# Sums of p.v as three additions and of pooled v as two, each in place of one strided pass, in a fused attention and two-layer kernel

## The chip, the cores and the metric

The kernel runs on one core of a Trainium2 chip. A core has a matrix engine (TensorE; PE in the profile), a vector engine (VectorE, DVE), a scalar engine (ScalarE, ACT), a general engine (GpSimd, POOL) and a queue for transfers (SyncE, SP). Each engine works through its own queue strictly in order. The metric is device time in microseconds (us), as a median over runs.

## The reference

Inputs are q, k and v of 4 batches, 8 heads, 576 positions and 64 dimensions. Cut to what matters:

```python
q_d, k_d, v_d = means of q, k, v over groups of 4 positions   # 144 positions
out_up    = repeat(softmax(q_d k_d^T / 8) v_d, 4)             # pooled attention
mask      = abs(i - j) < 4                                    # 7 neighbours
out_local = softmax(where(mask, q k^T / 8, -1e9)) v           # local attention
x = (out_up + out_local) as 2304 tokens x 512
h = x @ w_in                                                  # first layer, 2048 wide
x = (max(h, 0) + alpha * min(h, 0)) @ w_out
xn = x / sqrt(mean(x*x) + 1e-6) * rms_g                       # second layer, 1536 wide
out = (silu(xn @ w_gate) * (xn @ w_val)) @ w_out2
```

## The kernel before

The 2304 tokens are six blocks (m = 0 to 5) of 384, each of two groups of 192 tokens (g = 0 to 11). Every product of the two layers is made of three fp16 matmuls (high times high, high times low, low times high). `m1` runs the first layer on a block: per step f of 16, 24 matmuls of 384 columns (`hps` at L1368, `acc` at L1385), and on DVE the rows `hps` (L1374) and `ghl` (L374). `m2` runs the second layer: per step of 12, 24 matmuls for `gps` (L1485) and 9 for `oacc` (L1514), and on DVE `th` (L1496), `gps` (L1499) and `uhl` (L1506). ScalarE makes one pass between each of these. The blocks run in the order m1(0), m1(1), m2(0), m2(1), m1(2), m1(3), m2(2), m2(3), m1(4), m1(5), m2(4), m2(5).

The attention of a batch has to be done before the first layer takes its tokens, so it is fed as background tasks into the layers' steps. There are two ways of doing the local part. The first 768 tokens (groups 0 to 3) go over TensorE (the classes `Dense` and `DenseHead`). Groups 4 to 11 go over DVE and GpSimd, in `local_tasks`: positions lie in partitions, and six units per group (two positions times two heads of a pair each) are worked off one after another. For each unit, `mul_qk` multiplies q with seven neighbours' k (896 products per partition, tile `prod`), `red_qk` sums them over the dimension into `ls` (L489); after the softmax (`sm1`, `sm2`, last row L520) `mul_av` multiplies the weights with seven neighbours' v (L526, again 896 products in a `prod` tile), and `red_av` sums the seven into `lo` (L544). The products of units 0, 2 and 4 are made by GpSimd, those of units 1, 3 and 5 by DVE (the string "GVGVGV"). There are two buffers for `prod`, so a product waits until the unit two before it is summed. At the end `trans` turns `lo` over TensorE (`xps`, L560), adds the pooled attention (L573) and splits the sum into fp16 halves in `xt`.

The pooled attention of batch 0 is in `Dense.down`. Its first task, `smm`, sums four neighbouring rows of v (tile `sdv`, 72 partitions) into the part `pv` of a `dd` tile, with one reduction at L806. The other batches go through `down_tasks`, whose `pool` does the same with two additions (L632, L634).

The order of the queues isn't that of the code. `issue_order` (L24) takes all instructions, gives each a duration by a formula on its shape, and plans all engines forwards and backwards in 40 rounds; the order of the best round is laid on each engine. Its formula for DVE is 89 ns and a nanosecond or half of one per element, and 60 more for a scalar operand. The plan also lets a DVE instruction with two operands in SBUF and a GpSimd instruction wait for each other. So an edit of one instruction makes the order of all engines anew.

The two places that the change touches are, in the kernel before:

```python
add(st["o"][:, t:t + TP, j], pr[:, :, 0], pr[:, :, 2])            # L542, third of three, if av_pool
nc.vector.tensor_reduce(out=st["o"][:, t:t + TP, j],
    in_=pr.rearrange("p t n d -> p t d n"), axis=AX.X, op=ALU.add)  # L544, otherwise
def local(g, mul="GVGVGV", av=False, ...)                          # L1607: av is av_pool
```

Of the kernel before, what the change touches and what calls it, by code (L numbers as in the profile page):

```python
# [13 lines left out]
ALU = mybir.AluOpType  # L14
AX = mybir.AxisListType
# [240 lines left out]
def kernel(  # L256
# [14 lines left out]
    nc = tc.nc  # L271
    B, H, S, D = q.shape
# [23 lines left out]
    @contextmanager  # L296
    def together():
        n = len(nc.cur_bb.bb.instructions)
        yield
        groups.append([i.name for i in nc.cur_bb.bb.instructions[n:]])  # L300
# [413 lines left out]
    def pool_of(tag):  # L714
        return {"raw": raw_p, "xt": xt_p, "hl": hl_p, "ob": ob_p, "prod": prod_p, "at": ps_t, "w": ps_w}.get(
            tag) or (ps_a if tag in ("a0", "a1", "a2", "a3") else x1_p if tag[0] in "xr" and tag != "xs" else
                     wts if tag[0] in "uw" else att)

    class Dense:
# [78 lines left out]
        def down(self, h):  # L798
            st = self.st[h]

            def smm():
                t = st["qkp"]
                buf = prod_p.tile([SH, 4 * SD + 4 * D], F32, tag="prod", name="dd")
                a_ = buf[:, 0:4 * SD].rearrange("p (j a k) -> p j a k", j=2, a=2)
                st["pv"] = buf[:, 4 * SD:4 * SD + 4 * D].rearrange("p (j a d) -> p j a d", j=2, a=2)
                nc.vector.tensor_reduce(out=st["pv"].rearrange("p j a d -> p (j a) d"),  # L806
                                        in_=st.pop("v").rearrange("p (g r d) -> p g d r", g=4, r=4), axis=AX.X, op=ALU.add)
                ps = [pool_of(self.smp[j]).tile([128, 2, SD], F32, tag=self.smp[j], name="sps") for j in range(2)]
                with together():
                    for a in range(2):  # L810
                        for j in range(2):
                            nc.tensor.matmul(
                                ps[j][0:SH, a], t[j * 64:j * 64 + 64, 0, a * SH:(a + 1) * SH],
                                t[j * 64:j * 64 + 64, 1, :], start=True, stop=True)
                m = att.tile([SH, 2, 2], F32, tag=f"dm{h % 2}", name="dm")
                sm = att.tile([SH, 2, 2], F32, tag=f"dsum{h % 2}", name="dsum")
                for j in range(2):
                    nc.vector.tensor_reduce(out=m[:, j], in_=ps[j][0:SH], axis=AX.X, op=ALU.max, negate=True)
                nc.vector.tensor_scalar(out=m, in0=m, scalar1=1.0 / 16.0, scalar2=None, op0=ALU.mult)
                for j in range(2):  # L820
                    for a in range(2):
                        nc.scalar.activation(out=a_[:, j, a], in_=ps[j][0:SH, a], func=AF.Exp, scale=1.0 / 16.0,
                                             bias=m[:, j, a:a + 1], accum_out=sm[:, j, a:a + 1])
                st["a"], st["sum"] = a_, sm

            def nrm():
                a_, sm = st["a"], st["sum"]
                nc.vector.tensor_scalar(out=sm, in0=sm, scalar1=1e-9, scalar2=4.0, op0=ALU.add, op1=ALU.mult)
                nc.vector.reciprocal(sm, sm)
                nc.gpsimd.tensor_tensor(out=a_, in0=a_, in1=sm.unsqueeze(3).to_broadcast([SH, 2, 2, SD]),  # L830
                                        op=ALU.mult)

            def atr():
                t = att.tile([SH, 2, 2 * SD], F32, tag=("aT", "lo")[h % 2], name="aT")
                for j in range(2):
                    ps = ps_t.tile([128, 2 * SD], F32, tag="at", name="atps")
                    for kh in range(2):
                        for qh in range(2):
                            o = kh * SD + qh * SH
                            nc.tensor.transpose(ps[0:SH, o:o + SH], st["a"][:, j, qh, kh::2], ident[0:SH, 0:SH])  # L840
                    nc.scalar.activation(out=t[:, j], in_=ps[0:SH], func=AF.Copy)
                st["aT"] = t

            def avm():
                ps = ps_t.tile([128, SD], F32, tag="at", name="avps")
                with together():
                    for kh in range(2):
                        for j in range(2):
                            nc.tensor.matmul(ps[j * 64:j * 64 + 64, :], st["pv"][:, j, kh],
                                             st["aT"][:, j, kh * SD:(kh + 1) * SD], start=(kh == 0), stop=(kh == 1))  # L850
                if h == 0:
                    outd_t[self.b] = outd_p.tile([128, HP, SD], F32, tag="outd", name="outd")
                st["od"] = outd_t[self.b][:, h]
                nc.scalar.activation(out=st["od"], in_=ps, func=AF.Copy)

            return [smm, nrm, atr, avm]

        def local(self, c, h0, banks):
# [745 lines left out]
    def flush():  # L1604
        run(len(urgent), len(bg))

    def local(g, mul="GVGVGV", av=False, tags=(None, None, None), **kw):  # L1607
        return local_tasks(g, [V if c == "V" else G for c in mul], tags, av, **kw)

    def down(b, n=3, **kw):  # L1610
# [59 lines left out]
    def cut(l, at):  # L1670
# [8 lines left out]
        "o1": [],  # L1679
        "c3": pr2[2],  # L1680
        ("m2", 0): weave(pr2[3],local(4)),
        ("m2", 1): local(5)+down(2)+local(6),
        ("m1", 2): local(7)+local(8),
        ("m1", 3): down(3)+local(9),
        ("m2", 2): local(10),
# [57 lines left out]
```

## Time and profile before

| what | value |
|---|---|
| median of 3 runs | 993.3 us (991.09 to 995.36) |
| profiled execution | 989.59 us, its span 987.9 us |
| TensorE, weights of TensorE | 934.8 us (95%), 600.0 us (61%) busy |
| DVE, ScalarE, GpSimd | 695.7 (70%), 480.6 (49%), 117.1 us (12%) busy |
| transfers | 73.79 MB, 75 GB/s on average |

The span is the time from the first to the last instruction of one execution under the profiler. A row's duration runs from its start to its end; on DVE the next row starts a little before the last one ends, so the sum of durations is somewhat over the busy time. A matmul's duration contains its way through the array, so that 22 matmuls of 0.33 us each follow one another in 3.58 us. "Idle before" names what an engine waited for, as far as the semaphores show it.

### The profile page before, as it was taken

Reading aid. Unit: us, or ns where it says so; the run is one execution under the profiler, and the core shown is the slowest. Engines: PE = TensorE matmul, PEld = TensorE weight load, DVE = VectorE, ACT = ScalarE, POOL = GpSimd, SP = SyncE. Lnnn points to the kernel's source line nnn. Section 1 sums busy time; section 2 is a strip of 40 time slices with the busy share of each in tenths; the row PEclk is TensorE's granted clock in tenths of the full one; section 3 lists DMA queues with packets and bytes.
Section 4 is the critical chain, followed back from the end, with each engine's and each line's share of the span. In section 5 each row is a group of like instructions: output and inputs, shape, how many; then the busy total and the mean of one; then the engine's idle time right before and its main releaser. Section 6 shows DMA issues by size and latency. Waiting matters only on the chain.

```text
span 987.9 us, 16462 instructions
## 1 busy us (share of the span) xinstructions
PE 934.8 (95%) x6484; PEld 600.0 (61%) x6484; DVE 695.7 (70%) x1347; ACT 480.6 (49%) x1108; POOL 117.1 (12%) x96
## 2 busy tenths in 40 slices
PE   6978899999999999899899999989999999999998
PEld 4667777699655555455566555545556666555554
DVE  5689996888999977999976899953343353442333
ACT  5899889789753264233376322221232432321322
POOL 1101100300210202332201223300000000000000
PEclk9999999999999999999999999999999999999999
DMA  8866534565111133121122121010000000000000
GB/s 220 273 210 192 150 93 145 193 213 172 66 48 56 34 120 106 66 70 56 37 75 91 50 72 39 3 31 1 11 22 1 1 1 1 1 1 3 30 1 33
DMA packets 53711, 73.79 MB, mean 75 GB/s; under 512 B 22190, under 2 KB 35138, under 8 KB 53634
## 3 DMA queue, kind: packets, MB, share of 16 engines
q1 hardware_dynamic: 53634, 72.74, 24.2%
q8 instruction: 51, 0.84, 0.3%
q14 instruction: 26, 0.21, 0.1%
HBM read 68.01 MB, written 4.72 MB: 74 GB/s over the span
## 4 chain that ended last, share of the span: by engine, by line
PE 62%; DVE 18%; ACT 13%; DMA 4%; issue 3%; SPq 0%; ACTq 0%; DVEq 0%
PE gps L1485 20%; PE acc L1385 13%; PE hps L1368 12%; PE oacc L1514 9%; DVE lo L544 6%; DMA out_dram<-ob 3%; ACT wr L1107 2%; DVE prod L526 2%; ACT dls L897 2%; ACT wr L1110 1%; DVE gps L1499 1%; DVE hps L1374 1%; ACT g L1372 1%; ACT wi L373 1%; DVE ghl L374 1%
## 5 line engine op out<-in xcount | busy, mean ns | idle before, releaser
L1368 PE MATMUL hps<-xt,wi 128*128 128x192 f16 (+1 forms) x1536 | 342.7, 289 | 8.3 <-DVE ghl L374 5.1
L1485 PE MATMUL gps<-x,w 128*128 128x384 f16 x1728 | 341.2, 327 | 6.6 <-DVE th L1496 5.8
L1385 PE MATMUL acc<-ghl,wo 128*128 128x384 f16 (+1 forms) x960 | 246.0, 311 | 4.3 <-ACT ghl L373 3.2
L1485 PEld LDWEIGHTS <-w 128*128 128x128 f16 x1728 | 169.7, 99 | 120.8 <-issue 10.0
L1514 PE MATMUL oacc<-w,uhl 128*128 128x512 f16 x630 | 190.0, 379 | 1.7 <-ACT ob L1570 1.4
L1368 PEld LDWEIGHTS <-wi 128*128 128x128 f16 x1536 | 147.9, 100 | 57.0 <-issue 4.5
L1385 PEld LDWEIGHTS <-wo 128*128 128x128 f16 x1344 | 127.8, 98 | 67.0 <-issue 9.8
L1374 DVE SCALAR_TENSOR_TENSOR hps<-g,oma,hps 128x192 f32<-128x192 f32 (+1 forms) x128 | 65.9, 517 | 68.2 <-ACT g L1372 67.4
L1496 DVE SCALAR_TENSOR_TENSOR th<-th,gps 128x384 f32<-128x384 f32 x72 | 39.6, 551 | 96.5 <-ACT th L1494 96.1
L1514 PEld LDWEIGHTS <-uhl 128*128 128x128 f16 x630 | 61.9, 98 | 70.1 <-issue 4.8
L1494 ACT ACTIVATE th<-gps,tsc 128x384 f32<-128x384 f32 x72 | 41.7, 579 | 121.6 <-PE gps L1485 121.4
L1505 ACT ACTIVATE uhl<-gps 128x384 f16<-128x384 f32 x72 | 41.6, 578 | 109.0 <-DVE gps L1499 87.4
L1372 ACT ACTIVATE g<-hps 128x384 f32<-128x384 f32 x96 | 47.2, 492 | 91.8 <-PE hps L1368 91.3
L544 DVE TENSOR_REDUCE lo<-prod 128x128 f32<-128x896 f32 x48 | 82.4, 1719 | 0.0
L478 POOL TENSOR_TENSOR prod<-cq,ckv 128x896 f32<-128x896 f32 x24 | 52.3, 2179 | 198.4 <-DMA ckv<-in_k_dram 48.8
L373 ACT ACTIVATE ghl<-hps,grp 128x384 f16<-128x384 f32 (+1 forms) x73 | 42.1, 578 | 55.3 <-DVE hps L1374 54.1
L1385 PE MATMUL acc<-g,wo 128*128 128x384 f16 (+1 forms) x384 | 67.5, 286 | 0.0
L1506 DVE TENSOR_TENSOR uhl<-gps,uhl 128x384 f16<-128x384 f32 x72 | 45.3, 629 | 30.3 <-ACT uhl L1505 30.1
L526 POOL TENSOR_TENSOR prod<-ls,ckv 128x896 f32<-128x896 f32 x24 | 44.2, 1844 | 161.0 <-DVE lo L544 66.5
L374 DVE SCALAR_TENSOR_TENSOR ghl<-hps,grp,ghl 128x384 f16<-128x384 f32 (+1 forms) x73 | 44.3, 607 | 22.4 <-ACT ghl L373 22.2
L489 DVE TENSOR_REDUCE ls<-prod 128x14 f32<-128x896 f32 x48 | 51.1, 1074 | 0.0
L1107 ACT ACTIVATE wr<-wr 128x768 f32<-128x768 f32 (+1 forms) x48 | 42.2, 882 | 2.6 <-DMA wr<-in_moe_w_out_dram 2.6
(240 smaller groups left out, 1121.1 us busy)
## 6 DMA issues: line engine op xcount, KB each, us to landing
wr<-in_moe_w_out_dram SPq DMA_DIRECT2D x18, 512.0 KB
wr<-in_moe_w_in_dram SPq DMA_DIRECT2D x10, 768.0 KB
wr<-in_moe_w_gate_dram SPq DMA_DIRECT2D x8, 768.0 KB
wr<-in_moe_w_val_dram SPq DMA_DIRECT2D x8, 768.0 KB
ckv<-in_k_dram SPq DMA_DIRECT2D x7, 768.0 KB
ckv<-in_v_dram SPq DMA_DIRECT2D x7, 768.0 KB
wr<-in_moe_w_out_dram SPq DMA_DIRECT2D x20, 256.0 KB
sd<-in_q_dram SPq DMA_DIRECT2D x24, 144.0 KB
```

Source lines behind the costliest of these rows:

```text
L373: nc.scalar.activation(out=hi, in_=src, func=AF.Copy, scale=s)
L374: nc.vector.scalar_tensor_tensor(out=lo, in0=src, scalar=s, in1=hi, op0=ALU.mult, op1=ALU.subtract)
L478: engs[i].tensor_tensor(out=pr, in0=view(st["q"][:, j, t:t + TP], [[D, TP], [0, ND], [1, D]]), in1=view(st["k"][:, j, t:t + TP], [[D, TP], ...
L526: engs[i].tensor_tensor(out=pr, in0=view(st["s"][:, j, t:t + TP], [[ND, TP], [1, ND], [0, D]]), in1=view(st["v"][:, j, t:t + TP], [[D, TP] ...
L544: nc.vector.tensor_reduce(out=st["o"][:, t:t + TP, j], in_=pr.rearrange("p t n d -> p t d n"), axis=AX.X, op=ALU.add)
L1107: nc.scalar.activation(out=hi.bitcast(F32), in_=hi.bitcast(F32), func=AF.Prelu, scale=2.0 ** -112, alpha=2.0 ** 32)
L1368: nc.tensor.matmul(ps[:, j], wi[:, f + j, a, kk * 128:(kk + 1) * 128], x[:, b_, kk, c0:c0 + n], start=(i == 0), stop=(i == 3 * KK - 1))
L1372: nc.scalar.activation(out=g, in_=ps, func=AF.Relu, scale=-1.0)
L1374: nc.vector.scalar_tensor_tensor(out=ps[:, j], in0=g[:, j], scalar=oma[:, f + j:f + j + 1], in1=ps[:, j], op0=ALU.mult, op1=ALU.add)
L1385: nc.tensor.matmul(acc[e], wo_f(f)[:, a, e * 128:(e + 1) * 128], hl[:, b_], start=(f == f0 and i == 0), stop=(f == f1 and i == 2))
L1485: nc.tensor.matmul(ps, w2_t[i0 + f // 3].rearrange("p a (k c) -> p a k c", k=KK)[:, a, kk, (f % 3) * 128:(f % 3 + 1) * 128], xh[:, b_, kk] ...
L1514: nc.tensor.matmul(acc[tt], t[:, a, tt * 128:(tt + 1) * 128], w[:, b_, f % 3], start=(f in first and i == 0), stop=(f in last and i == 2))
```

## The change

Three things are edited. `local` has `av=True` as its default, so `red_av` takes its first branch: in the product tile of seven slices of 64, slices 0 to 2 get slices 3 to 5 added (384 elements per partition), then slices 0 and 2 get slices 1 and 6 added (256), and the third addition writes slice 0 plus slice 2 into `lo` (128). All three read two operands in SBUF. In `Dense.down` the reduction L806 becomes two additions, of 512 and of 256 elements per partition, the first in place in the tile of v. And since the instructions are others, the order is planned anew. Lines after L806 have numbers that are higher by three in the kernel after.

```diff
-                nc.vector.tensor_reduce(out=st["pv"].rearrange("p j a d -> p (j a) d"),
-                                        in_=st.pop("v").rearrange("p (g r d) -> p g d r", g=4, r=4), axis=AX.X, op=ALU.add)
+                vt = st.pop("v").rearrange("p (g r) -> p g r", g=4)
+                nc.vector.tensor_tensor(out=vt[:, :, 0:2 * D], in0=vt[:, :, 0:2 * D], in1=vt[:, :, 2 * D:4 * D],
+                                        op=ALU.add)
+                nc.vector.tensor_tensor(out=st["pv"].rearrange("p j a d -> p (j a) d"), in0=vt[:, :, 0:D],
+                                        in1=vt[:, :, D:2 * D], op=ALU.add)
...
-    def local(g, mul="GVGVGV", av=False, tags=(None, None, None), **kw):
+    def local(g, mul="GVGVGV", av=True, tags=(None, None, None), **kw):
```

What `red_av` now runs stands in both kernels:

```python
add = lambda o, a, c: nc.vector.tensor_tensor(out=o, in0=a, in1=c, op=ALU.add)
add(pr[:, :, 0:3], pr[:, :, 0:3], pr[:, :, 3:6])
add(pr[:, :, 0:3:2], pr[:, :, 0:3:2], pr[:, :, 1:7:5])
add(st["o"][:, t:t + TP, j], pr[:, :, 0], pr[:, :, 2])
```

The first place where the order is shown is DVE's queue in the fourth of the eight groups (g = 7, inside m1(2)). Of the kernel before, from unit 1's product on; `prod_5473`, `prod_5506`, `prod_5510` and `prod_5513` are units 0 to 3, and the rows L526 are the products that DVE makes itself:

```order
L526 TENSOR_TENSOR prod_5506<-ls_5367,ckv_5432 128x896
L544 TENSOR_REDUCE lo_5508<-prod_5473 128x2x64
L374 SCALAR_TENSOR_TENSOR xt_5295<-xs_5302,sc_104,xt_5295 128x4x96
L544 TENSOR_REDUCE lo_5508<-prod_5506 128x2x64
L1374 SCALAR_TENSOR_TENSOR hps_5517<-g_5530,oma_102,hps_5517 128x384
L526 TENSOR_TENSOR prod_5513<-ls_5367,ckv_5432 128x896
L544 TENSOR_REDUCE lo_5508<-prod_5510 128x2x64
L374 SCALAR_TENSOR_TENSOR ghl_5516<-hps_5517,grp_115,ghl_5516 128x384
L544 TENSOR_REDUCE lo_5508<-prod_5513 128x2x64
```

And of the kernel after, where `prod_5513`, `prod_5546`, `prod_5552` and `prod_5557` are units 0 to 3 (L1377 is L1374 of before):

```order
L526 TENSOR_TENSOR prod_5546<-ls_5407,ckv_5472 128x896
L539 TENSOR_TENSOR lo_5548<-prod_5513 128x2x64
L539 TENSOR_TENSOR prod_5546<-prod_5546 128x2x192
L374 SCALAR_TENSOR_TENSOR ghl_5515<-hps_5516,grp_115,ghl_5515 128x384
L1377 SCALAR_TENSOR_TENSOR hps_5563<-g_5576,oma_102,hps_5563 128x384
L539 TENSOR_TENSOR prod_5546<-prod_5546 128x2x2x64
L539 TENSOR_TENSOR prod_5552<-prod_5552 128x2x192
L539 TENSOR_TENSOR lo_5548<-prod_5546 128x2x64
L539 TENSOR_TENSOR prod_5552<-prod_5552 128x2x2x64
L526 TENSOR_TENSOR prod_5557<-ls_5407,ckv_5472 128x896
```

Each sum has become three rows, and between them stand rows of the first layer (`hps`, `ghl`). The second row of the later piece is the third addition of unit 0, which frees the buffer for GpSimd's product of unit 2.

The second place is the end of the last group's sums (g = 11, inside m2(3)), DVE's queue. Before:

```order
L526 TENSOR_TENSOR prod_7957<-ls_7617,ckv_7758 128x896
L1499 SCALAR_TENSOR_TENSOR gps_7554<-th_7551,kap_119,gps_7554 128x384
L544 TENSOR_REDUCE lo_7862<-prod_7912 128x2x64
L1506 TENSOR_TENSOR uhl_7568<-gps_7554,uhl_7568 128x384
L544 TENSOR_REDUCE lo_7862<-prod_7957 128x2x64
```

After, where L1499, L1502 and L1509 are the rows L1496, L1499 and L1506 of before:

```order
L526 TENSOR_TENSOR prod_8053<-ls_7705,ckv_7846 128x896
L1499 SCALAR_TENSOR_TENSOR th_7771<-th_7771,gps_7758 128x384
L539 TENSOR_TENSOR lo_7950<-prod_8006 128x2x64
L1502 SCALAR_TENSOR_TENSOR gps_7774<-th_7771,kap_119,gps_7774 128x384
L539 TENSOR_TENSOR prod_8053<-prod_8053 128x2x192
L539 TENSOR_TENSOR prod_8053<-prod_8053 128x2x2x64
L1509 TENSOR_TENSOR uhl_7788<-gps_7774,uhl_7788 128x384
L539 TENSOR_TENSOR lo_7950<-prod_8053 128x2x64
```

There are three rows of the second layer between the last own product and the last write of `lo`, where two stood before. GpSimd's queue keeps its products in the same sequence.

## Rows read from the trace of the kernel before

**Rows 1.** The page, busy time of each engine, and DVE in 40 slices.
```profile
PE 934.8 (95%) x6484; PEld 600.0 (61%) x6484; DVE 695.7 (70%) x1347; ACT 480.6 (49%) x1108; POOL 117.1 (12%) x96
...
DVE  5689996888999977999976899953343353442333
```

**Rows 2.** Three stretches: length; busy PE, PEld, DVE, ACT, POOL; clock; transfers' share; GB/s.
```profile
0.00:235.00 235.00, 211.55 (x2062) 174.18 (x2063) 190.65 (x473) 201.36 (x512) 26.61 (x50) 0.99 0.62 187
235.00:655.00 420.00, 396.85 (x2515) 238.26 (x2513) 382.00 (x652) 183.88 (x423) 90.47 (x47) 1.00 0.21 64
655.00:987.90 332.90, 326.44 (x1912) 187.52 (x1909) 123.07 (x225) 95.31 (x174) 0.00 (x0) 1.00 0.03 9
```

**Rows 3.** The same for eight stretches, one per group: second, third, last, sum.
```profile
320.50:342.50 22.00, 20.36 (x119) 11.64 (x117) 22.00 (x32) 3.72 (x7) 5.18 (x3) 1.00 0.07 21
397.20:418.00 20.80, 18.20 (x101) 9.54 (x100) 20.68 (x23) 3.98 (x8) 8.03 (x5) 1.00 0.15 52
...
631.50:652.00 20.50, 17.80 (x100) 9.62 (x98) 20.23 (x23) 5.09 (x9) 5.07 (x3) 1.00 0.10 26
sum 200.60, PE 178.59 PEld 108.20 DVE 194.68 ACT 78.63 POOL 56.05; mean PE 22.32 PEld 13.53 DVE 24.34 ACT 9.83 POOL 7.01
```

**Rows 4.** DVE in order of time in the third group: start, length, row.
```profile
398.58 1.68 DVE L526 TENSOR_TENSOR prod<-ls,ckv 128x896 f32<-128x896 f32 x1
400.18 1.71 DVE L544 TENSOR_REDUCE lo<-prod 128x128 f32<-128x896 f32 x1
401.81 0.61 DVE L1499 SCALAR_TENSOR_TENSOR gps<-th,kap,gps 128x384 f32<-128x384 f32 x1
402.34 1.73 DVE L544 TENSOR_REDUCE lo<-prod 128x128 f32<-128x896 f32 x1
403.99 0.54 DVE L1506 TENSOR_TENSOR uhl<-gps,uhl 128x384 f16<-128x384 f32 x1
```

**Rows 5.** TensorE at the end of that group, idle before in brackets.
```profile
417.62 0.32 PE L1368 MATMUL hps<-xt,wi 128*128 128x384 f16 x1 [2.32 <-DVE ghl L374]
```

**Rows 6.** Groups by line and shape: count | busy us, mean ns | idle before.
```profile
L544 DVE TENSOR_REDUCE lo<-prod 128x128 f32<-128x896 f32 x48 | 82.4, 1719 | 0.0
...
L632 DVE TENSOR_TENSOR sd<-sd 72x512 f32<-72x512 f32 x36 | 25.2, 699 | 4.6 <-ACT dd L619 4.6
...
L1299 DVE TENSOR_TENSOR ra<-ra 128x384 f32<-128x384 f32 x15 | 8.3, 553 | 1.1 <-ACT ra L1294 1.1
...
L806 DVE TENSOR_REDUCE dd<-sdv 72x256 f32<-72x1024 f32 x4 | 7.7, 1936 | 0.0
...
L573 DVE TENSOR_TENSOR xs<-xps,outd 128x128 f32<-128x128 f32 x16 | 6.0, 373 | 0.0
...
L634 DVE TENSOR_TENSOR dd<-sd 72x256 f32<-72x256 f32 x12 | 5.0, 417 | 0.0
```

**Rows 7.** The chain of waits in the first 60 us, shares by line.
```profile
by line: PE lsps L877 10.4%; PE tps L792 9.9%; ACT T L793 9.2%; ACT dls L897 8.0%; ACT dls L912 6.5%; ACT dd L822 6.3%; PE atps L840 6.1%; ACT wr L1107 6.0%; DMA wo<-in_q_dram 5.8%; PE sps L812 5.6%; SPq L743 4.4%; PE avps L849 4.1%; PE lsp
```

**Rows 8.** GpSimd in order of time: two p.v products.
```profile
401.97 1.69 POOL L526 TENSOR_TENSOR prod<-ls,ckv 128x896 f32<-128x896 f32 x1 [2.66 <-DVE lo L544]
...
468.94 1.94 POOL L526 TENSOR_TENSOR prod<-ls,ckv 128x896 f32<-128x896 f32 x1 [9.48 <-issue]
```

**Rows 9.** DVE in order of time beside the second of them.
```profile
468.72 0.61 DVE L374 SCALAR_TENSOR_TENSOR xt<-xs,sc,xt 128x384 f16<-128x384 f32 x1
469.25 1.91 DVE L634 TENSOR_TENSOR qkp<-sd 72x256 f32<-72x256 f32 x1
```

**Rows 10.** The chain of waits after 655 us, in order of time: start, length, matmuls.
```profile
656.51 3.58 PE gps L1485 x22
```

## Prediction

> **What bounds the kernel now.** I read the page first. TensorE is busy 934.8 of 987.9 us and VectorE (DVE) 695.7, but DVE's share is not even: mostly eight or nine tenths in the first 26 slices, three to five after them [rows 1]. So I cut the span at 235 and 655 us, where the local attention begins and ends [rows 2]. After 655 us TensorE is idle 6.5 of 332.9 us with DVE at 123: nothing on DVE is worth anything there. From 235 to 655 us TensorE is idle 23.2 of 420 us, and DVE is busy 382. Before 235 us TensorE is idle 23.5 us, but ScalarE is busy 201 of those 235, and DVE only 190.7.
>
> Then I looked for where the 23.2 us lie. Eight stretches, one for each group of p.v products (from the softmax's last multiplication L520 to a few us after the last sum into `lo`), hold 22.0 us of it: they are 200.6 us long, TensorE is busy 178.6 in them, DVE 194.7 [rows 3]. In the fourth line of such a stretch DVE does nothing but products, sums of 1.7 us and single rows of the dense layers, without a gap [rows 4], and at its end TensorE sits 2.32 us until DVE's `ghl` of the next step is there [rows 5]. So in these eight places DVE sets the time: what reaches TensorE is the number of DVE rows of the dense layers ("main rows" here: L1374, L374 `ghl`, L1496, L1499, L1506) that the queue lets through between local rows.
>
> **What goes and what comes, in DVE time.** L544 takes 1.719 us, 48 times: 82.4 us [rows 6]. In its place stand three additions over 384, 256 and 128 elements per partition. An addition of 384 with both inputs in SBUF is L1299, 553 ns; of 256, L634 `dd`, 417 ns [rows 6]. None of 128 with both inputs in SBUF is there: on the line through these two (136 ns for 128 elements) it is 281 ns, and the 128-element L573, which writes with a stride, took 373. I take 281, since the new rows have runs of 64 as L634's neighbours have, and keep 373 as the other end. Sum 1.251 us, 0.468 less per unit, 22.5 us over 48 units (18.0 with 373). A DVE row starts 0.07 to 0.08 us before the one ahead of it ends (401.81 against 400.18 + 1.71) [rows 4], so two more rows per unit could give up to 0.16 us each back where neighbours don't depend on each other: 7.7 us at most, which I put into the block sums below.
>
> L806 goes from 1.936 us to 699 (L632, 512 elements) plus 417 ns, 0.82 us, four times: 3.3 us [rows 6]. These lie in the first 50 us, where the chain goes through TensorE transposes and ScalarE and names no L806 [rows 7]. What comes late there is ScalarE, which the edit doesn't touch: 0 to 1 us, taken as 0.
>
> **The price: GpSimd.** L544 reads one operand, and it runs beside GpSimd's product at its usual length: 402.34 to 404.07, 1.73 us, while the product ran from 401.97 to 403.66 [rows 4, 8]. DVE rows with two operands in SBUF do not: the L634 at 469.25 took 1.91 us where 0.42 is usual, and ended 0.28 us after GpSimd's product (468.94 + 1.94) did [rows 8, 9]. That product had been released while L374 `xt` was running; it got in between two DVE rows that stand directly behind one another. So GpSimd wins at the next row's border, and DVE then waits for the rest of the product, 1.69 us, except while it has rows that read PSUM to do.
>
> All three additions are of the kind that waits. By the Trainium skill (SBUF — State Buffer, Who interferes with whom) a tensor_reduce never takes the port that VectorE shares with GpSimd, and a tensor_tensor with two SBUF inputs blocks against GpSimd's reads; the trace agrees with both in the rows just named. By that rule alone each of the 24 products costs DVE up to its length; the third rival below works that out from rows.
>
> I counted this from the order, product by product. A p.v product starts when its buffer is free, after the third addition of the unit two before it; I then add what DVE has to do without the port before its next row that needs it, and take the rest of 1.69 us (2.08 for a q.k product) as a wait. In the fourth block the second product is covered by two main rows (`ghl`, `hps`: 1.23 us, 0.46 left), the third by one (1.08 left), the next group's first product by one (1.57 left), and the first has only 0.28 of cover. Over 24 p.v products and the seven first q.k products behind them the waits come to 38.2 us in the new order; the same count on the old order gives 13.4, because there a sum of 1.72 us covers nearly each product. So 24.8 us of new waits stand against 22.5 us of saved work: DVE's time alone is a draw.
>
> **Where the gain is.** The new order puts more main rows into a block. From L520 to the last write of `lo`, over eight blocks, DVE's rows (each by its mean, less 0.075 for the overlap) sum to 172.6 us before and 142.8 after, waits not counted. Of main rows there stand six before and seven after in the fourth block, six and twelve in the eighth. A step of a dense layer is 24 matmuls of 0.163 us (3.58 us for 22 [rows 10]), 3.9 us for two main rows; in the second layer 5.8 us for three: each main row feeds TensorE for 1.95 us (a half-wide one for half). I set against each block's length and waits what its main rows feed. Before, the eight blocks are short by 9.9, 6.5, 3.7, 5.7, 8.2, 5.8, 5.8 and 6.7 us, 52.3 in all, of which TensorE showed 22.0 as idle (the rest was in buffers ahead), a share of 0.42. After: 5.8, 8.5, 0.9, 4.6, 6.9, 5.4, 2.5 and 0 (the eighth has 4.9 us too many, which can't be saved up), 34.6 in all. (52.3 - 34.6) x 0.42 = 7.4 us.
>
> The sum: -7.4 (blocks), 0 (pooled v), 0 (after 655 us). The profiled execution took 989.6 us (span 987.9 and 1.7 around it), so 982.2 for one like it. The median of the runs shown is 993.3, 3.7 above; I carry the difference over: **986 us**. Ends: with 373 ns for the small addition and no overlap gained, 12.2 us of DVE work come back, at 0.42 a loss of 5 us of the 7.4 (991); if the share that shows is one instead of 0.42, 17.7 us of gain (976). Elsewhere the order is new too: I take nothing for that and allow 4 us either way.
>
> **Rivals.**
> 1. *The waits eat it, no change.* The draw in DVE time holds, and the extra main rows only stand in the queue, not ready when GpSimd holds the port. For: the new waits (24.8) exceed the saving (22.5). Against: the eighth and seventh blocks, where the feed exceeds or nearly meets the length. Price: 0 to 3 us of gain, 990 to 993.
> 2. *All of the blocks' idle time goes*: the feed is enough once the sums no longer hold the queue for 1.7 us at a stretch. Price 22 us less, 971. For: the seventh and eighth blocks; against: the second, short by 8.5 us against 6.5.
> 3. *Slower: GpSimd gets in at each border and nothing covers it.* The place is the pair of units in a block: the third addition frees the buffer, GpSimd starts, the next addition waits in DVE's in-order queue, and the main rows behind it wait with it, and TensorE for them. Without any cover 24 x 1.69 + 7 x 2.08 = 55.1 us of waits, 41.7 more than before, less 22.5: 19 us more on DVE in the blocks, at 0.42 to 1 of it 8 to 19 us, 1001 to 1012. It decides where a product costs over 0.73 us more than before (22.5 / 31); my count has 0.80, so only the main rows' places hold it off. Against: rows of the dense layers do stand behind most products.
>
> **Chances.** Forecast 0.42 (0.37 of it more than 0.5% faster, 0.05 within), rival 1 0.25, rival 2 0.11, rival 3 0.22 (0.21 slower). About 0.5%, 5 us, is what a measurement of this kernel can tell from no change. So faster 0.48, within 0.5% 0.31, slower 0.21. The forecast's own range is 976 to 991; the range to 973 and 1003 takes in rival 1, most of rival 2 and the lower part of rival 3.
>
> **What would show it.** Right: the new rows at about 553, 417 and 281 ns where GpSimd is quiet, 1.7 to 2.3 us in a number of them beside its products; TensorE idle in the eight stretches down from 22 to some 15 us, the eighth's 2.7 us gone, the second's not; from 655 us on nothing changed. Wrong: the means of the three additions summing to over 2 us (rival 3), or TensorE's idle time in the blocks as before with DVE as full (rival 1); a change of the time before 235 us by more than 4 us would mean that the new order, not the sums, made it.

## The result and the profile after

The changed kernel takes 967.5 us in the median (967.3 to 969.0), the kernel before 992.2 (988.4 to 995.4); the ratio is 0.976, with a 95% interval of 0.972 to 0.979. The forecast was 986 us with a range of 973 to 1003: the direction was right, the size a third of what came. Of the rivals the second, with 971 us, is nearest in number.

The page of the kernel after, busy time of each engine over a span of 965.8 us; it answers to [rows 1]:

```profile
PE 929.6 (96%) x6484; PEld 600.2 (62%) x6484; DVE 685.5 (71%) x1447; ACT 481.7 (50%) x1108; POOL 117.5 (12%) x96
```

DVE's busy time fell by 10.2 us only, the span by 22.1. The same three stretches as in [rows 2], kernel after (length; busy PE, PEld, DVE, ACT, POOL; clock; transfers):

```profile
0.00:235.00 235.00, 212.77 (x2098) 177.75 (x2099) 192.59 (x485) 205.44 (x516) 26.56 (x50) 0.96 0.63 189
235.00:655.00 420.00, 412.58 (x2605) 247.15 (x2604) 376.54 (x750) 184.71 (x426) 90.91 (x46) 1.00 0.21 64
655.00:965.80 310.80, 304.28 (x1786) 175.28 (x1784) 116.35 (x213) 91.55 (x167) 0.00 (x0) 1.00 0.03 8
```

From 235 to 655 us TensorE is idle 7.4 us instead of 23.2, and after 655 us as long as before (6.5 us). To place the gain I counted through TensorE's main matmuls (`hps`, `acc`, `gps`, `oacc`, 783 us of columns at 2.4 GHz, the same in both kernels) and noted when 120 and 480 us of them had been reached. Before these were 246.4 and 669.8 us of the span, after 243.5 and 647.7. So 2.9 us came from the start, 19.2 from the stretch of the local attention ("the local stretch" from here on: 423.4 us before, 404.2 after), and nothing from the rest, 318.1 us in both.

In that stretch the eight groups' windows, chosen as for [rows 3]; second, third, last and sum:

```profile
311.00:333.00 22.00, 20.38 (x118) 11.45 (x117) 22.00 (x46) 4.70 (x12) 5.12 (x3) 1.00 0.07 22
384.00:405.00 21.00, 21.00 (x119) 11.41 (x118) 20.08 (x36) 4.15 (x8) 9.26 (x5) 1.00 0.12 38
...
622.50:645.00 22.50, 22.24 (x129) 12.43 (x128) 18.74 (x37) 6.14 (x11) 5.06 (x3) 1.00 0.12 34
sum 200.00, PE 194.96 PEld 120.53 DVE 187.07 ACT 82.13 POOL 58.79; mean PE 24.37 PEld 15.07 DVE 23.38 ACT 10.27 POOL 7.35
```

TensorE is idle 5.0 us in them instead of 22.0. The second still loses 1.6 us, the last 0.3 of its 2.7.

The new rows by shape in the kernel after (count | busy us, mean ns | idle before); they answer to L544 and L806 in [rows 6]:

```profile
L539 DVE TENSOR_TENSOR prod<-prod 128x256 f32<-128x256 f32 x48 | 31.4, 653 | 0.0
L539 DVE TENSOR_TENSOR prod<-prod 128x384 f32<-128x384 f32 x48 | 29.1, 607 | 4.3 <-POOL prod L526 4.3
L539 DVE TENSOR_TENSOR lo<-prod 128x128 f32<-128x128 f32 x48 | 18.3, 381 | 0.0
...
L807 DVE TENSOR_TENSOR sdv<-sdv 72x512 f32<-72x512 f32 x4 | 2.6, 668 | 0.0
L809 DVE TENSOR_TENSOR dd<-sdv 72x256 f32<-72x256 f32 x4 | 1.7, 415 | 0.4 <-PE avps L852 0.4
```

The three means sum to 1.641 us, against 1.719 for L544. That is the draw in DVE's time which the prediction had. The waits for GpSimd are in these means. A piece of DVE's time in the fourth group, and GpSimd beside it, show one:

```profile
428.37 0.54 DVE L539 TENSOR_TENSOR prod<-prod 128x384 f32<-128x384 f32 x1
428.84 0.60 DVE L374 SCALAR_TENSOR_TENSOR ghl<-hps,grp,ghl 128x384 f16<-128x384 f32 x1
429.37 1.84 DVE L539 TENSOR_TENSOR prod<-prod 128x256 f32<-128x256 f32 x2
431.14 0.28 DVE L539 TENSOR_TENSOR lo<-prod 128x128 f32<-128x128 f32 x1
```

```profile
428.59 1.88 POOL L526 TENSOR_TENSOR prod<-ls,ckv 128x896 f32<-128x896 f32 x1 [2.63 <-DVE lo L539]
```

GpSimd's product was released at 428.5 us, while an addition was running, and took 1.88 us instead of the 1.69 of [rows 8]; I read the difference as its wait for that addition's end. The next two additions, 0.41 and 0.54 us long when quiet, took 1.84 us together. Only `ghl` covered part of the product, as counted for this place. Over the whole trace, DVE rows that lie beside a GpSimd row and last over 0.15 us more than the median of their kind are 17 before, with 14.9 us too much, and 38 after, with 37.8. The prediction had 13.4 and 38.2 from the order.

### The profile page after: what moved, and what is told of

Same layout as the page of the kernel before. It is cut to its first block, busy times and chain, and to the rows that moved or that the text cites. A ratio compares the mean times of both kernels' runs of the same rounds, so it can differ in the third digit from the quotient of the medians.

```text
span 965.8 us, 16581 instructions
## 1 busy us (share of the span) xinstructions
PE 929.6 (96%) x6484; PEld 600.2 (62%) x6484; DVE 685.5 (71%) x1447; ACT 481.7 (50%) x1108; POOL 117.5 (12%) x96
## 4 chain that ended last, share of the span: by engine, by line
PE 67%; DVE 13%; ACT 9%; issue 6%; DMA 5%; POOL 0%; SPq 0%; ACTq 0%; POOLq 0%
PE gps L1488 23%; PE hps L1371 12%; PE acc L1388 12%; PE oacc L1517 11%; DMA out_dram<-ob 4%; DVE prod L539 2%; DVE ls L489 1%; ACT wr L1110 1%; ACT dls L900 1%; DVE prod L526 1%; ACT wr L1113 1%; ACT wi L373 1%; DVE ghl L374 1%; DVE prod L478 1%; DVE hps L1377 1%
## 5 line engine op out<-in xcount | busy, mean ns | idle before, releaser
L1371 PE MATMUL hps<-xt,wi 128*128 128x192 f16 (+1 forms) x1536 | 357.0, 290 | 7.2 <-DVE g L374 3.8
L1388 PE MATMUL acc<-ghl,wo 128*128 128x384 f16 (+1 forms) x960 | 253.8, 310 | 1.7 <-DVE ghl L374 0.6
L1377 DVE SCALAR_TENSOR_TENSOR hps<-g,oma,hps 128x192 f32<-128x192 f32 (+1 forms) x128 | 66.0, 516 | 61.3 <-ACT g L1375 61.0
L1499 DVE SCALAR_TENSOR_TENSOR th<-th,gps 128x384 f32<-128x384 f32 x72 | 39.6, 550 | 87.8 <-ACT th L1497 87.4
L478 POOL TENSOR_TENSOR prod<-cq,ckv 128x896 f32<-128x896 f32 x24 | 54.8, 2284 | 191.6 <-DVE ls L489 50.6
L1388 PE MATMUL acc<-g,wo 128*128 128x384 f16 (+1 forms) x384 | 70.4, 286 | 0.0
L1509 DVE TENSOR_TENSOR uhl<-gps,uhl 128x384 f16<-128x384 f32 x72 | 45.3, 629 | 28.1 <-ACT uhl L1508 27.8
L526 POOL TENSOR_TENSOR prod<-ls,ckv 128x896 f32<-128x896 f32 x24 | 43.6, 1816 | 163.3 <-DVE lo L539 70.6
L539 DVE TENSOR_TENSOR prod<-prod 128x384 f32<-128x384 f32 (+1 forms) x96 | 59.4, 630 | 4.3 <-POOL prod L526 4.3
```

What stands on the lines that cost most here:

```text
L478: engs[i].tensor_tensor(out=pr, in0=view(st["q"][:, j, t:t + TP], [[D, TP], [0, ND], [1, D]]), in1=view(st["k"][:, j, t:t + TP], [[D, TP], ...
L526: engs[i].tensor_tensor(out=pr, in0=view(st["s"][:, j, t:t + TP], [[ND, TP], [1, ND], [0, D]]), in1=view(st["v"][:, j, t:t + TP], [[D, TP] ...
L539: add = lambda o, a, c: nc.vector.tensor_tensor(out=o, in0=a, in1=c, op=ALU.add)
L1371: nc.tensor.matmul(ps[:, j], wi[:, f + j, a, kk * 128:(kk + 1) * 128], x[:, b_, kk, c0:c0 + n], start=(i == 0), stop=(i == 3 * KK - 1))
L1377: nc.vector.scalar_tensor_tensor(out=ps[:, j], in0=g[:, j], scalar=oma[:, f + j:f + j + 1], in1=ps[:, j], op0=ALU.mult, op1=ALU.add)
L1388: nc.tensor.matmul(acc[e], wo_f(f)[:, a, e * 128:(e + 1) * 128], hl[:, b_], start=(f == f0 and i == 0), stop=(f == f1 and i == 2))
```

## The experiments

DVE's time was a draw, as forecast, and still the local stretch got 19 us shorter. Two theories were set against each other. A: the gain comes from the plan. `issue_order` gives L544 89 + 896 / 0.96 ns = 1.02 us, where it takes 1.72, or 1.64 less the overlap with the next row. The three additions get 1.07 us in the plan, and take 1.01 us from start to next start when nothing is beside them (469, 336 and 202 ns), and the plan knows that they and GpSimd exclude each other. So before, each of 48 sums ran some 0.6 us over, TensorE's queue had been laid out for rows that came later, and it stood at its head waiting. B: the gain comes from the rows: short ones let main rows through earlier.

Every kernel was timed beside the kernel before on its chip. The table gives the ratio to it with its interval, TensorE's idle time from 235 to 655 us, the waits for GpSimd as above, and the local stretch and the time of its first mark, found as above. These four columns come from one profiled execution of each kernel, while the executions of one kernel lie 1.3 to 7.8 us apart; that of e9 was the slowest of its four (982.9 us).

| kernel | us | ratio (95%) | idle, us | GpSimd waits, us | first mark, us | local stretch, us |
|---|---|---|---|---|---|---|
| before | 992.2 | 1 | 23.2 | 14.9 | 246.4 | 423.4 |
| e7: before, order shifted | 995.1 | 1.004 (1.002 to 1.007) | 24.8 | 17.6 | 252.6 | 422.0 |
| e3: pooled v only | 987.6 | 0.996 (0.994 to 0.997) | 21.3 | 13.3 | 250.5 | 417.6 |
| e1: before, planned right | 978.5 | 0.987 (0.985 to 0.989) | 12.2 | 15.9 | 250.6 | 406.9 |
| e9: as e1, order shifted | 979.2 | 0.986 (0.982 to 0.990) | 13.2 | 16.5 | 253.0 | 410.0 |
| after | 967.5 | 0.976 (0.972 to 0.979) | 7.4 | 37.8 | 243.5 | 404.2 |
| e8: after, order shifted | 972.9 | 0.983 (0.979 to 0.986) | 9.0 | 43.3 | 251.9 | 400.7 |
| e12: after, 160 rounds | 972.7 | 0.980 (0.976 to 0.985) | 7.1 | 39.3 | 249.6 | 402.0 |
| e2: p.v only | 979.1 | 0.987 (0.985 to 0.990) | 10.2 | 40.5 | 254.4 | 404.8 |
| e4: after, planned short | 983.4 | 0.993 (0.990 to 0.995) | 15.7 | 43.4 | 249.0 | 412.4 |
| e10: after, planned long | 980.2 | 0.987 (0.984 to 0.991) | 13.2 | 30.4 | 252.0 | 407.8 |
| e6: after, plan blind to GpSimd | 975.6 | 0.985 (0.981 to 0.988) | 13.6 | 39.8 | 248.7 | 409.4 |
| e5: both kinds of sums | 975.1 | 0.984 (0.980 to 0.988) | 10.1 | 16.1 | 246.4 | 409.7 |
| e11: as e5, order shifted | 975.5 | 0.983 (0.979 to 0.986) | 12.3 | 10.1 | 246.6 | 410.6 |

**The sums as they were, planned with what they take (e1, e9).** On the kernel before:

```diff
         if e == "DVE":
...
+            if i.opcode == "TensorReduce" and list(ins[0].ap)[-1][0] > 1:
+                return 89 + 1.81 * n
```

> The kernel before with its strided sums L544 and L806 unchanged; only the planner's formula is told what they take (89 ns + 1.81 ns per element: 1.71 us where it had 1.02). Theory A (the gain of the changed kernel comes from an order planned with a duration that holds; before, each of 48 sums ran 0.7 us over its plan and TensorE waited for the main rows queued behind): most of the gain, 968 to 978 us, TensorE idle from 235 to 655 us about 10 us instead of 23. Theory B (the gain comes from the rows: three short rows let main rows through earlier, and some DVE time is saved): 988 to 996 us, the idle time stays above 18 us.

e1 measured 978.5 us, half a microsecond over A's range and far from B's. No instruction of the program differs from the kernel before, only their order. The engines' busy time in e1, the p.v sum's group (where two lines more shift the numbers by two) and the row for 235 to 655 us:

```profile
PE 933.9 (96%) x6484; PEld 601.0 (62%) x6484; DVE 695.8 (71%) x1347; ACT 480.8 (49%) x1108; POOL 116.8 (12%) x96
```

```profile
L546 DVE TENSOR_REDUCE lo<-prod 128x128 f32<-128x896 f32 x48 | 82.4, 1721 | 0.0
```

```profile
235.00:655.00 420.00, 407.78 (x2584) 245.45 (x2582) 385.42 (x656) 186.93 (x429) 87.83 (x46) 1.00 0.22 66
```

The sum takes 1.721 us, DVE is busy 695.8 us, as in [rows 1], and TensorE is idle 12.2 us instead of 23.2. What changed is who waits for it. TensorE's waits for DVE (us in total, times, longest), of the kernel before and then of e1:

```profile
PE gps L1485 <- DVE th L1496: 5.8, 6, 1.6
PE hps L1368 <- DVE ghl L374: 5.1, 5, 2.3
PE xps L560 <- DVE lo L544: 4.0, 5, 1.3
```

```profile
PE hps L1370 <- DVE ghl L376: 2.3, 5, 0.8
```

`th` is not among e1's twelve longest waits of TensorE (0.5 us), and `ghl` has halved with a longest of 0.8 us instead of 2.3. That is A's picture. The second order of the same work:

```diff
-            return 89 + n / (1.92 if fast else 0.96) + 60 * (extra > 0)
+            return 91 + n / (1.92 if fast else 0.96) + 60 * (extra > 0)
```

> The kernel before with its strided sums, planned with their measured length (as e1) and with 91 ns instead of 89 as DVE's fixed cost: a second order of the same work. Theory A (a plan that holds): 972 to 984 us, the stretch of the local attention some 405 to 411 us long as in e1 (406.9). Theory B (the short rows give the gain, and e1 was a lucky order): 985 to 995 us, that stretch above 415 us.

979.2 us, a local stretch of 410.0, and from 235 to 655 us:

```profile
235.00:655.00 420.00, 406.80 (x2584) 245.16 (x2582) 383.80 (x654) 185.48 (x428) 88.32 (x46) 0.99 0.22 66
```

So e1 was no lucky order, and B alone is out.

**What another order does by itself (e7, e8, e12).** e7 is the kernel before and e8 the changed one, both with 91 in place of 89 as just shown; e12 is the changed one with more rounds:

```diff
-def issue_order(tc, nc, groups, rounds=40):
+def issue_order(tc, nc, groups, rounds=160):
```

> The kernel before, planned with 91 ns instead of 89 as DVE's fixed cost: nothing changes but the order. It measures what another order alone does. Theory A: 986 to 996 us, TensorE idle from 235 to 655 us still above 18 us, since the sums still run 0.7 us over their plan. If the gain was luck of one order: anything from 968 to 1000 us.

> The changed kernel, planned with 91 ns instead of 89 as DVE's fixed cost. Theory A: 964 to 974 us, the gain stays. If it was luck of one order: 975 to 992 us.

> The changed kernel with 160 planning rounds instead of 40, from which the planner keeps the best by its own reckoning. Theory A, if its reckoning is good to a per cent: 962 to 972 us. If between plans that hold the rest is luck of the start (243 to 254 us up to the same point): 965 to 978 us.

They came to 995.1, 972.9 and 972.7 us, e7 and e8 within A's ranges and e12 0.7 us over it. Their rows for 235 to 655 us, in that sequence:

```profile
235.00:655.00 420.00, 395.22 (x2520) 238.38 (x2520) 384.07 (x660) 185.01 (x427) 86.91 (x47) 1.00 0.21 65
```

```profile
235.00:655.00 420.00, 411.00 (x2618) 248.58 (x2616) 380.98 (x752) 187.78 (x429) 88.76 (x46) 1.00 0.21 65
```

```profile
235.00:655.00 420.00, 412.91 (x2638) 249.34 (x2637) 377.73 (x755) 187.90 (x430) 89.78 (x46) 1.00 0.21 64
```

In the local stretch the kinds don't mix: three orders with sums planned short lie at 417.6 to 423.4 us, two with sums planned right at 406.9 and 410.0, four with additions at 400.7 to 404.8. TensorE's idle time between the two marks, which leaves the start out, says the same: 17.7 to 22.5 us with sums planned short, 8.5 and 9.4 planned right, 5.2 to 6.9 with additions. The first mark, though, wanders between 243.5 and 254.4 us with no relation to the kind. The changed kernel has the earliest mark of all; e8, e12 and e2 have as short a local stretch, or a shorter one, and are 5 to 12 us slower because they start later. More planning rounds did not help.

**Each part alone (e2, e3).** e2 is the kernel before with only `av=True`, e3 with only the two additions of pooled v.

> The kernel before with only the sums of p.v as three additions; pooled v stays one reduction. A and B both: 965 to 972 us, within 3 us of the changed kernel, since pooled v lies in the first 50 us where the chain goes over ScalarE. If pooled v (and the start's order) carried part of it: 975 to 985 us.

> The kernel before with only pooled v as two additions; the sums of p.v stay one reduction. A and B both: no change but that of a new order, 987 to 995 us. If the start carried it: 975 to 985 us.

e2 took 979.1 us, outside what both theories had and within the range for pooled v or the start's order carrying a part. Its local stretch is that of the changed kernel (404.8 us), its start 10.9 us later. e3's 987.6 us is just clear of no change; its local stretch is 5.8 us shorter though nothing in it was edited, and its start 4.1 later. So pooled v has no price or gain of its own that these runs can tell from that of another order: 3.4 us of DVE's time were saved (7.7 less 2.6 and 1.7), in a stretch in which other orders move the time by up to 11 us.

**The additions, planned wrong (e4, e10, e6).** In the changed kernel, for the additions of p.v alone:

```diff
+            if any(str(x.tensor.name).startswith("prod") for x in ins) and i.opcode == "TensorTensor" and n < 896:
+                return 0.51 * (89 + n / 0.96)
```

> The changed kernel; only the planner is told that the three additions take half of its formula (0.54 us for a unit instead of 1.07; a quiet unit takes 1.25), so that each unit again runs 0.7 us over its plan as L544 did. Theory A: most of the gain goes, 980 to 992 us, TensorE idle from 235 to 655 us above 15 us. Theory B: 965 to 972 us.

983.4 us, as A had it: idle time back to 15.7 us, with the same rows as the changed kernel. From start to next start this plan is 0.47 us a unit short (0.54 against 1.01), that of the sums was 0.6. The opposite error, a factor of 1.58 in place of 0.51:

> The changed kernel; the planner is told that the three additions take 1.58 times its formula (1.69 us a unit instead of 1.07), too long by as much as the sums were too short. Theory A, if a plan must hold both ways: 975 to 985 us. If only a plan that is too short hurts (main rows queued behind local ones), 965 to 974 us. Theory B: 965 to 972 us.

980.2 us, within A's range, though its ratio is also that of e2, which is planned right. The four orders planned right have a local stretch of 402.9 us in the mean; e10 has 407.8, e4 412.4. So a plan that is too long seems to cost too, half as much. But this is one order, and part of its stretch is TensorE's clock (below), so it isn't shown. And the plan without its knowledge that additions and GpSimd exclude each other:

```diff
         n = len([a for a in ins if free(a) > 1 and not psum(a)])
+        if n > 1 and str(ins[0].tensor.name).startswith("prod") and free(ins[0]) < 896:
+            return False
```

> The changed kernel; only the planner no longer knows that the additions wait for GpSimd (and make it wait). Theory A: some of the gain goes, since some 25 us of waits are then outside the plan: 973 to 985 us. Theory B: 965 to 971 us.

975.6 us, which A had, but the four orders planned right take as long (967.5 to 979.1). Only the local stretch, 409.4 us, and the idle time, 13.6 us, are above all of theirs (404.8 and 10.2 at most), in one order. The rows of e4, e10 and e6 for 235 to 655 us:

```profile
235.00:655.00 420.00, 404.26 (x2569) 243.83 (x2568) 379.84 (x752) 186.71 (x428) 90.74 (x47) 1.00 0.21 64
```

```profile
235.00:655.00 420.00, 406.84 (x2591) 245.67 (x2589) 367.72 (x743) 189.14 (x429) 84.61 (x46) 0.99 0.22 67
```

```profile
235.00:655.00 420.00, 406.37 (x2593) 245.07 (x2591) 378.87 (x756) 189.55 (x431) 89.05 (x46) 1.00 0.22 68
```

e10 has the least DVE time of the three, 367.7 us in that window and 680.5 over the span (685.5 in the changed kernel), and more idle time of TensorE than the changed kernel.

**Both kinds of sums (e5, e11).** Additions only where GpSimd made the product; where DVE made it, the one reduction, planned with its measured length, which can run beside GpSimd's next product. e11 is the same with 91 for 89.

```diff
-            if av_pool:
+            if av_pool and engs[i] is nc.gpsimd:
```

> The changed kernel, but only the units whose product GpSimd makes are summed by three additions; those whose product DVE makes keep the one reduction, which can run beside GpSimd's next product, and the planner has that reduction's measured length. Theory A (a plan that holds is what counts, DVE time is secondary): 964 to 972 us, about the changed kernel. Theory B (the short rows give the gain): half of it, 975 to 985 us. If the waits for GpSimd (37.8 us in the changed kernel against 14.9 before) are what is left to win: 955 to 963 us, with the waits under 25 us.

> As e5 (additions for GpSimd's units, one reduction for DVE's, planned with its measured length), with 91 ns instead of 89: a second order. If fewer waits for GpSimd are worth time beyond the plan: 960 to 968 us and a shorter stretch than the changed kernel's 404 us. Theory A (DVE's time is secondary): 967 to 979 us, that stretch 402 to 411 us.

975.1 and 975.5 us. e5 is 3 us over A's range and at the foot of B's; e11 is within A's, which was set higher after e5. The waits for GpSimd fall as meant, to 16.1 and 10.1 us, and DVE is busy 4 to 7 us less from 235 to 655 us than in the changed kernel (376.5):

```profile
235.00:655.00 420.00, 409.89 (x2604) 247.01 (x2602) 372.41 (x714) 188.60 (x431) 86.83 (x47) 0.99 0.22 66
```

```profile
235.00:655.00 420.00, 407.74 (x2572) 244.99 (x2570) 369.93 (x713) 190.07 (x432) 90.78 (x47) 0.99 0.22 67
```

But the local stretch is 409.7 and 410.6 us, as long as with sums alone that are planned right. A part of that is TensorE's clock, which was granted at 1.2 instead of 2.4 GHz for a while, as here in e11 (clock 0.50), behind waits of TensorE of 2.5 and 1.7 us:

```profile
332.10:338.90 6.80, 5.71 (x23) 2.96 (x24) 6.80 (x18) 3.14 (x13) 0.00 (x0) 0.50 0.35 108
489.10:492.50 3.40, 3.40 (x12) 1.61 (x11) 3.02 (x14) 1.59 (x5) 0.00 (x0) 0.50 0.28 83
```

That is 10.2 us of e11's local stretch; in e5, e9 and e10 it is 6.8, in after, e8 and e12 nothing. At half the clock up to half of it is lost, by my estimate from these lengths 5.1 us in e11 and 3.4 in the others. Less that, e5 and e11 have 406.3 and 405.5 us, still as long as e1 and e9 so reckoned (406.0 and 406.6) and longer than any of the four orders of the additions planned right. So fewer waits for GpSimd and less DVE time didn't turn into time here. No kernel of these beats the changed one.

## Why the prediction was wrong, point by point

**What bounds the kernel** was right. The gain that isn't the start's lies in the local stretch, 19.2 us, of which 15.6 are idle time of TensorE; after 655 us nothing moved.

**DVE's time** was right in its sum. The additions were taken at 553, 417 and 281 ns; the trace has medians of 545, 411 and 277 where GpSimd is quiet. New waits were counted at 24.8 us and measured at 22.9, against 22.5 us forecast as saved. What two additions waited beside the product at 428.59 us, 0.97 us, had been counted as 1.08.

**The step that failed** is "(52.3 - 34.6) x 0.42 = 7.4 us". Measured, TensorE's idle time fell by 15.8 us and the local stretch by 19.2. What was wrong in it is the 0.42, the share of the blocks' shortage that shows as idle time, carried over from the kernel before. In the eight stretches after, 5.0 of the 34.6 us showed, a share of 0.14. The same count on e1's order gives a shortage of 48.5 us, close to the 52.3 of the kernel before, and e1 is idle 12.2 us instead of 23.2. With the blocks' lengths as the traces have them, the count gives 49 to 54 us in the three orders with sums planned short, 47 and 52 with sums planned right, 29 to 36 with additions; the idle time from 235 to 655 us is 0.44 to 0.47 of that in the first, 0.26 in the second, 0.24 to 0.35 in the third. So the rows did lower the shortage, as forecast, and what the runs put in place of a fixed share is whether the plan's durations hold, for which the prediction had no term.

The section on the kernel before had the formula, and the rows of L544 had 1.72 us; I used the formula only to say that the order would be new, and did not set the two beside each other. Sums planned right make the local stretch 12.5 us shorter (mean of e1 and e9, 408.5, against 421.0, the mean of before, e7 and e3). Additions instead of sums, both planned right, take off another 5.5 us (mean of after, e8, e12 and e2, 402.9). That is two thirds for the plan and a third for the rows; the second figure is about as large as the spread within a kind (up to 6 us), so its size is rough; in time, the four orders of the additions have ratios of 0.976 to 0.987 and the two of sums planned right 0.987 and 0.986.

**Elsewhere** I had taken 0, and 4 us either way. The changed kernel gained 2.9 us in the start; over all orders the first mark spans 11 us, so this allowance was too small, and the measured 22.1 us of span owe some of their size to a good start: three other orders of the same p.v additions came to 972.7 to 979.1 us.

**The rivals.** The first (the waits eat the gain) had its premise measured, and fell: DVE's time was nearly a draw and the time was not. The third (nothing covers GpSimd) fell: the waits were as counted, and TensorE's idle time fell beside them. That this is because the plan knew of them rests on one order: where it did not (e6), the idle time was 13.6 us instead of 7.4. The second had the number but another reason: not that sums of 1.7 us held up the queue, but mostly that they held it up unplanned. The place that I had named against it, the second block, kept its 1.6 us as foreseen.

**What stays open:** why short rows give the last 5 us (a smaller shortage is the likely reason), and why half of them (e5, e11), with as small a shortage (31 and 32 us by the traces' lengths) but a share of 0.32 and 0.40, give none of it. The length of single rows was not varied by itself, a plan too long for the sums was not tried, and e4, e6 and e10 are one order each.

## What to carry to other kernels

Where an order is planned from a formula, set the formula's duration of every frequent row beside the trace's before judging an edit: one row that runs 0.6 us over its plan, 48 times, cost about twice what the shorter rows gave on top (12.5 us against a rough 5.5), and correcting the formula alone brought 1.3%. Here saved engine time and saved waits bought nothing (e5, e11), while an accurate duration did; that a wait which the plan knows is cheaper than the same wait outside it, one order suggests (e6). And a new order moves the time by itself (here by up to 11 us in the start), so run a second order of the same work before crediting an edit with a per cent.
